# Transposing q and k on TensorE in halves of 64 columns instead of 128, in attention fused with a GEGLU block

## The chip, the cores and the metric

The kernel runs on one core of a Trainium2 chip. The metric is the device time of one launch in microseconds; the time before is the median of three runs.

## The reference

The program computes sliding-window attention with a linear distance bias (ALiBi), and then a GEGLU feed-forward block on its output. Batch 8, 8 heads, 576 positions, head size 64; 4608 tokens of width 512, hidden width 1536. All inputs and the output are float32.

```
scores = scale * q @ k.T                     # scale = 1 / sqrt(64)
mask   = (rel >= 0) & (rel < 128)            # rel = query position - key position
scores = where(mask, scores - slope[h] * |rel|, -1e9)
attn   = softmax(scores)
x      = (attn @ v), as (B*S, H*D)           # 4608 x 512
out    = (gelu(x @ w_gate) * (x @ w_val)) @ w_out
```

## The kernel before

The order of all instructions on all engines is written out by hand (a manual schedule). Everything is kept in bf16, products accumulate in float32 in PSUM, which is used as a pool of eight banks that are handed out in turn (`bank()`): a bank is free again when what reads it has finished, eight requests later.

**The feed-forward block** runs over nine groups of 512 tokens (`g`). For each group `gate_val` makes twelve hidden blocks (`f`): four matmuls with `wg` and four with `wv` (line 625, 512 moving columns each) into two banks, then ACT takes the gelu (L632) and DVE multiplies (L633). `out_part` multiplies the hidden blocks with `wo` (L662).

**Attention** for batch g+2 is set between these matmuls. POOL issues the loads of q and k (`load_qk`, L112); the sequence of a batch lies in five row blocks: four of 128 rows and one of 64 (`rows(j)`, 576 = 4 x 128 + 64), with the heads side by side, so that 128 columns are a pair of heads `c`. Scores need q and k with the head dimension on partitions. `transposes(b, c)` does this for one pair of heads: for q and for k it takes a bank, transposes the five row blocks into it (L178; the data is the weight operand and the identity moves through the array), and copies 128 x 576 elements to `qT` or `kT` (L181), q on ACT and k on DVE, but both on DVE for two pairs. One such run of five transposes is called a group here. There are 48: batches 2 to 7, four pairs, q and k.

The groups are called in blocks between other TensorE work: usually two calls, that is four groups, after a `gate_val`, with another `gate_val` behind it (f = 5 and 7 of g = 1, and f = 6 and 8 of g = 2 to 5). The first half of batch 3 follows f = 11 of g = 1, and the second half is two calls in the list of steps of g = 1 (two groups each); behind these three blocks stand scores (`score`, L209).

Batches 0 and 1 go other ways. Batch 1 is loaded in runs of rows (`RUNS`: 128 partitions with three rows each, 96 partitions with two) and is transposed by `transpose_runs` (L154), which takes 64 columns at a time and writes the two heads of a pair to rows 0 to 63 and 64 to 127 of a bank. The scores (L209, L291) and the products with the values (L494) use a quarter of the array each, 64 rows by 64 columns; the sums of L430 use 128 rows by 32 columns.

Of the kernel before, what the change touches and what calls it, by code (L numbers as in the profile page):

```python
# [32 lines left out]
def kernel(  # L33
# [10 lines left out]
    nc = tc.nc  # L44
# [23 lines left out]
    def bank():  # L68
        return psum.tile([128, 512], FP32, name="ps")
# [11 lines left out]
    ident = consts.tile([128, 128], BF16, name="ident")  # L81
# [20 lines left out]
    def rows(j):  # L102
        return 64 if j == 4 else 128
# [69 lines left out]
    def transposes(b, c, copies=None):  # L173
        for w, (src, dst, copy) in enumerate(zip((qs, ks), (qT, kT), copies or (act, dve))):
            ps = bank().bitcast(BF16)
            for j in range(5):
                n = rows(j)
                nc.tensor.transpose(  # L178
                    out=ps[:, 128 * j:128 * j + n], in_=src[b % 2][0:n, j, 128 * c:128 * c + 128],
                    identity=ident[0:n, 0:n])  # L180
            copy(out=dst[b % 2][:, c, 0:S], in_=ps[:, 0:S])  # L181


# [533 lines left out]
    for h in (0, 2, 4, 6):  # L717
        for w, src in ((0, q), (1, k)):
            (nc.scalar if w and h == 0 else nc.sync).dma_start(  # L719
                out=raw[w][h // 4].rearrange("p (h x) -> p h x", h=4)[:, h % 4:h % 4 + 2, :],  # L720
                in_=src[0][h:h + 2, 0:384, :].rearrange("h (p r) d -> p h (r d)", r=3))
# [115 lines left out]
    for do in inverse_a:  # L837
        do[1]()
    dve(out=pairs1.rearrange("p x (h d) -> p h x d", d=64),
        in_=vb[1].rearrange("p j x -> p (j x)")[:, 0:1536].rearrange(  # L840
            "p (h x d) -> p h x d", h=H, x=3))
# [46 lines left out]
    for n in range(4):  # L888
        nc.gpsimd.dma_start(
            out=wo[:, 3 * n:3 * n + 3, :],  # L890
            in_=moe_w_out[384 * n:384 * n + 384, :].rearrange("(c p) f -> p c f", p=128))
# [26 lines left out]
    def exp_table():  # L918
        nc.scalar.preload_act_table_set("natural_log_exp_and_others")

    RUN = {"s": scores, "s2": scores2, "add": add, "sum4": sums4, "gather": gather, "spread": spread_dma, "pv": values, "pv+": values_and_sums,
           "masks": flush, "table": exp_table, "transposes": transposes, "last": out_last, "scale": lambda: scales.pop()(), "o": out_half}

    for g in range(NG):
        for f in range(9 if g == 0 else 0, NF):
            gate_val(g, f)
            if g == 1 and f in (5, 7):
                transposes(2, f - 5)
                transposes(2, f - 4)
# [71 lines left out]
```

## Time and profile before

| | |
|---|---|
| median of 3 runs | 361.32 us (360.48 to 361.93) |
| the profiled execution | 361.49 us, its span 359.7 us |
| TensorE (PE) busy | 349.9 us, 97% of the span |
| its weight loads (PEld) | 184.7 us |
| DVE busy | 203.4 us |
| ACT busy | 184.4 us |
| L178: transposes of batches 2 to 7 | 240 in 13 blocks, between 68.3 and 241.4 us |
| L154: transposes of batch 1 | 80 in one block, at 36.6 us |

A row of the groups view reads: line, engine, operation, tile written <- tiles read, the part of the array (rows * columns) where it is a matmul or a weight load, the moving operand's shape, count, then busy time in us and the mean duration of one in ns, then idle time of the engine before them. A matmul's duration runs from its start to its last result, and matmuls overlap: the distance between two starts is what one costs. A piece of the chain reads: start, length, what, how many instructions.

### The profile page before, as it was taken

Reading aid. Unit: us, or ns where it says so; the run is one execution under the profiler, and the core shown is the slowest. Engines: PE = TensorE matmul, PEld = TensorE weight load, DVE = VectorE, ACT = ScalarE, POOL = GpSimd, SP = SyncE. Lnnn points to the kernel's source line nnn. Section 1 sums busy time; section 2 is a strip of 40 time slices with the busy share of each in tenths; the row PEclk is TensorE's granted clock in tenths of the full one; section 3 lists DMA queues with packets and bytes.
Section 4 is the critical chain, followed back from the end, with each engine's and each line's share of the span. In section 5 each row is a group of like instructions: output and inputs, shape, how many; then the busy total and the mean of one; then the engine's idle time right before and its main releaser. Section 6 shows DMA issues by size and latency. Waiting matters only on the chain.

```text
span 359.7 us, 8537 instructions
## 1 busy us (share of the span) xinstructions
PE 349.9 (97%) x3508; PEld 184.7 (51%) x3556; DVE 203.4 (57%) x382; ACT 184.4 (51%) x340; POOL 105.6 (29%) x139
## 2 busy tenths in 40 slices
PE   8999999999999999999999999999999999999996
PEld 6667556555654555454545554455544544444444
DVE  7887865445789546944596458844694413302420
ACT  7964786447696437544473439253753123313322
POOL 6965689406700086004900192004000000000000
PEclk9999999999999999999999999999999999999999
DMA  8999999908950099219990599049203320011002
GB/s 210 171 197 191 200 187 187 124 2 52 162 107 2 5 194 189 64 23 135 170 122 5 131 138 181 3 104 105 81 31 69 95 89 2 0 58 60 0 28 90
DMA packets 118043, 35.65 MB, mean 99 GB/s; under 512 B 101716, under 2 KB 110964, under 8 KB 118004
## 3 DMA queue, kind: packets, MB, share of 16 engines
q0 software_dynamic: 107456, 18.10, 65.2%
q1 hardware_dynamic: 7232, 10.75, 8.5%
q10 hardware_dynamic: 3316, 6.25, 7.9%
q8 instruction: 28, 0.46, 0.5%
q14 instruction: 11, 0.09, 0.1%
HBM read 43.65 MB, written 9.53 MB: 148 GB/s over the span
## 4 chain that ended last, share of the span: by engine, by line
PE 94%; DMA 1%; issue 1%; DVE 1%; ACT 1%; SPq 0%; DVEq 0%
PE ps L625 52%; PE ps L662 24%; PE ps L178 6%; PE ps L494 5%; PE ps L291 2%; PE ps L682 2%; PE ps L209 1%; DMA qs<-in_q_dram 1%; PE ps L430 1%; PE ps L698 1%; PE ps L154 1%; ACT P L222 0%; SPq L719 0%; DVE xT L530 0%; DVE qT L162 0%
## 5 line engine op out<-in xcount | busy, mean ns | idle before, releaser
L633 DVE TENSOR_TENSOR hT<-ps,gelu 128x512 bf16<-128x512 f32 (+3 forms) x117 | 73.8, 646 | 97.6 <-PE ps L625 91.3
L632 ACT ACTIVATE gelu<-ps 128x512 bf16<-128x512 f32 (+3 forms) x117 | 65.1, 564 | 98.5 <-PE ps L625 96.2
L625 PE MATMUL ps<-xT,wg 128*128 128x512 bf16 (+4 forms) x460 | 112.1, 361 | 0.8
L625 PE MATMUL ps<-xT,wv 128*128 128x512 bf16 (+4 forms) x460 | 111.2, 361 | 0.4
L662 PE MATMUL ps<-wo,hT 128*128 128x512 bf16 x374 | 87.6, 380 | 2.1 <-issue 1.4
L625 PEld LDWEIGHTS <-wv 128*128 128x128 bf16 x472 | 45.0, 98 | 48.7
L625 PEld LDWEIGHTS <-wg 128*128 128x128 bf16 x472 | 43.5, 98 | 45.8
L662 PEld LDWEIGHTS <-hT 128*128 128x128 bf16 x396 | 37.0, 98 | 43.3
L222 ACT ACTIVATE P<-ps 128x512 bf16<-128x512 f32 (+1 forms) x108 | 51.3, 583 | 3.9 <-PE ps L209 3.6
L225 DVE TENSOR_TENSOR P<-P,emask 128x768 bf16<-128x768 bf16 x60 | 31.2, 556 | 19.5 <-ACT P L222 17.7
L667 ACT COPY osb<-ps 128x512 f32<-128x512 f32 x27 | 15.9, 588 | 51.3 <-PE ps L662 51.3
L112 POOL DMA_DIRECT2D vb<-in_v_dram x40 | 34.0, 902 | 2.9 <-DMA wo<-in_moe_w_out_dram 1.0
L956 POOL COPY mark<-hT 1x2 bf16<-1x2 bf16 x4 | 0.7, 174 | 108.4 <-DVE hT L633 108.4
L112 POOL DMA_DIRECT2D qs<-in_q_dram x30 | 25.5, 870 | 4.9 <-DMA wo<-in_moe_w_out_dram 2.7
L112 POOL DMA_DIRECT2D ks<-in_k_dram x30 | 25.4, 893 | 0.3 <-PE ps L625 0.3
L181 ACT COPY qT<-ps 128x576 bf16<-128x576 bf16 x22 | 14.0, 638 | 9.8 <-PE ps L178 9.8
L494 PE MATMUL ps<-P,vb 64*64 64x192 bf16 (+2 forms) x752 | 17.7, 221 | 0.6 <-issue 0.4
L558 DVE TENSOR_TENSOR xT<-ps,rb 128x512 bf16<-128x512 f32 (+3 forms) x34 | 14.7, 502 | 4.6 <-PE ps L494 4.6
L494 PEld LDWEIGHTS <-vb 64*64 64x64 bf16 x752 | 14.7, 107 | 4.0 <-issue 3.0
L181 DVE COPY kT<-ps 128x576 bf16<-128x576 bf16 x24 | 11.0, 457 | 5.7 <-PE ps L178 5.1
L378 DVE TENSOR_TENSOR T<-P 64x1024 bf16<-64x1024 bf16 x20 | 13.7, 686 | 0.6
L178 PE MATMUL ps<-ident,ks 128*128 128x128 bf16 (+1 forms) x120 | 12.7, 218 | 0.0
(95 smaller groups left out, 238.0 us busy)
## 6 DMA issues: line engine op xcount, KB each, us to landing
out_dram<-osb SPq DMA_DIRECT2D x35, 256.0 KB, 3.1
rb<-rd ACTq DMA_DIRECT2D x10, 576.0 KB, 6.4
vb<-in_v_dram POOLq DMA_DIRECT2D x32, 128.0 KB, 6.3
qs<-in_q_dram POOLq DMA_DIRECT2D x24, 128.0 KB, 4.5
ks<-in_k_dram POOLq DMA_DIRECT2D x24, 128.0 KB, 6.1
wo<-in_moe_w_out_dram POOLq DMA_DIRECT2D x4, 384.0 KB, 12.3
wg<-in_moe_w_gate_dram POOLq DMA_DIRECT2D x5, 256.0 KB, 8.4
wv<-in_moe_w_val_dram POOLq DMA_DIRECT2D x5, 256.0 KB, 8.9
```

The lines of the kernel that those rows point to most:

```text
L112: nc.gpsimd.dma_start(out=t[at:at + n, j, :].rearrange("p (h d) -> p h d", h=H), in_=src[b][:, 128 * j:128 * j + n, :].rearrange("h p d -> ...
L178: nc.tensor.transpose(out=ps[:, 128 * j:128 * j + n], in_=src[b % 2][0:n, j, 128 * c:128 * c + 128], identity=ident[0:n, 0:n])
L181: copy(out=dst[b % 2][:, c, 0:S], in_=ps[:, 0:S])
L222: nc.scalar.activation(out=dst, in_=src, func=AF.Exp, scale=0.125)
L225: nc.vector.tensor_tensor(out=dst, in0=dst, in1=m, op=ALU.mult)
L494: mm = nc.tensor.matmul(out=out, lhsT=lhsT, rhs=prob(b)[half, c, i, col:col + q1 - q0], start=all(t[2] != u for t in todo[:n]), stop=True, ...
L558: nc.vector.tensor_tensor(out=xT[:, c, at:at + e - a], in0=src, in1=recip[b][:, c, a:e], op=ALU.mult)
L625: nc.tensor.matmul(out=ps[:, a:e], lhsT=w[:, c, 128 * f:128 * (f + 1)], rhs=xT[:, c, t0 + lo + a:t0 + lo + e], start=begins and a == 0, st ...
L632: nc.scalar.activation(out=gl[:, 0:n], in_=pg, func=AF.Gelu)
L633: nc.vector.tensor_tensor(out=hid[g][:, f, lo:hi], in0=pv, in1=gl[:, 0:n], op=ALU.mult)
L662: nc.tensor.matmul(out=acc[g], lhsT=hid[g][:, f, 128 * t:128 * (t + 1)], rhs=wo[:, f, :], start=(f == 0), stop=(f == NF - 1))
L667: (nc.vector.tensor_copy if g < B - 2 and t in by_dve.get(g, (0,)) else nc.scalar.copy)(out=osb, in_=acc[g])
```

## The change

For each row block, the one transpose of 128 columns becomes two of 64: head 2c goes to output rows 0 to 63 and head 2c+1 to rows 64 to 127. The same values land at the same places of the bank. The copies behind, the banks and the waits stay.

```diff
             ps = bank().bitcast(BF16)
             for j in range(5):
                 n = rows(j)
-                nc.tensor.transpose(
-                    out=ps[:, 128 * j:128 * j + n], in_=src[b % 2][0:n, j, 128 * c:128 * c + 128],
-                    identity=ident[0:n, 0:n])
+                for i in (0, 1):
+                    at = 128 * c + 64 * i
+                    nc.tensor.transpose(
+                        out=ps[64 * i:64 * i + 64, 128 * j:128 * j + n],
+                        in_=src[b % 2][0:n, j, at:at + 64], identity=ident[0:n, 0:n])
             copy(out=dst[b % 2][:, c, 0:S], in_=ps[:, 0:S])
```

## The prediction

> **What bounds the kernel now.** I read the page's busy shares first, then its clock row and its chain.
>
> ```profile
> PE 349.9 (97%) x3508; PEld 184.7 (51%) x3556; DVE 203.4 (57%) x382; ACT 184.4 (51%) x340; POOL 105.6 (29%) x139
> ...
> PEclk9999999999999999999999999999999999999999
> ...
> PE 94%; DMA 1%; issue 1%; DVE 1%; ACT 1%; SPq 0%; DVEq 0%
> PE ps L625 52%; PE ps L662 24%; PE ps L178 6%; PE ps L494 5%; PE ps L291 2%; PE ps L682 2%; PE ps L209 1%; DMA qs<-in_q_dram 1%; PE ps L430 1%; PE ps L698 1%; PE ps L154 1%; ACT P L222 0%; SPq L719 0%; DVE xT L530 0%; DVE qT L162 0%
> ```
>
> TensorE is busy 97% of the span at full clock and carries 94% of the chain; the two engines that empty PSUM are at 57% and 51%. The changed line, L178, is itself 6% of the chain. So what is added to or taken from TensorE in these blocks goes to the end nearly one to one. The busy column cannot say how much, since matmuls overlap: what counts is the distance from one start to the next.
>
> Next the groups by shape. L178 is the edited line; L154, batch 1's transposes, already writes 64 columns to each half of the output rows, so it is the nearest row to the new code.
>
> ```profile
> L178 PE MATMUL ps<-ident,ks 128*128 128x128 bf16 x96 | 9.5, 222 | 0.0
> L178 PE MATMUL ps<-ident,ks 64*128 64x64 bf16 x24 | 4.8, 200 | 0.0
> ...
> L154 PE MATMUL ps<-ident,qs 128*64 128x128 bf16 x24 | 1.4, 220 | 0.0
> L154 PE MATMUL ps<-ident,qs 96*64 96x96 bf16 x16 | 1.0, 205 | 0.0
> ```
>
> The first pair of numbers is the part of the array (rows * columns), the second the moving operand. A group of L178 is four transposes of shape 128*128 and one of shape 64*128 for the last 64 rows of a batch. L154 has no 64-row shape: batch 1 is loaded in runs of 128 and 96 rows.
>
> Then the chain in order of time, one block of each:
>
> ```profile
> 36.66 2.17 PE ps L154 x80
> ...
> 68.71 1.74 PE ps L178 x20
> ```
>
> L154 does eight groups (576 columns of 128 each) in 2.17 us, 0.27 us a group; L178 does four in 1.74 us, 0.43 us a group. On this view alone the edit would save 0.16 us in each of 48 groups, about 8 us. The timeline of TensorE's weight loads tells why L178 is slow:
>
> ```profile
> 68.86 0.09 PEld L178 LDWEIGHTS <-qs 64*128 64x128 bf16 x1
> 69.00 0.10 PEld L178 LDWEIGHTS <-ks 128*128 128x128 bf16 x1
> ...
> 36.59 0.11 PEld L154 LDWEIGHTS <-qs 128*64 128x64 bf16 x2 [0.42 <-issue]
> ```
>
> The fourth 128-row transpose of this group starts at 68.717. The load for the 64-row one starts 147 ns later, though loads elsewhere in the group start one step ahead; the next group's first load again waits 132 ns. The third line is the same wait where the array goes from L625's 128*128 to L154's 128*64. The starts of a group in L178 are 67, 56, 56, 151 and 132 ns apart, 462 in all, and 283 of that is going into and out of the 64-row shape. The 128-row transposes come every 56 ns; L154's pairs also come every 55 to 56 ns, the second of a pair 2 to 5 ns after the first. A pair does the work of one old transpose, so **for 128-row blocks the edit gains nothing**.
>
> **The change part by part.** *The shape switch.* I went through every place in the trace where the shape of the array changes between two matmuls, and took the distance between their starts:
> - 128*128 to 64*128 (rows only) after 128 moving columns: 150 to 151 ns, 48 times
> - 64*128 to 128*128 after 64 columns: 129 to 133
> - 64*128 to 64*64 (columns only) after 64 columns: 129 to 130 (L178 to L209), 121 (L790 to L494)
> - 64*64 to 128*128: 121 to 123 after 64 columns where nothing else is waited for, 149 after 128
> - 128*128 to 64*64, 128*32 or 128*64 after 512 columns: 308 to 310, against 216 without a change
> - 96*64 to 128*128 after 96 columns: 137.
>
> Subtract the streaming time (216 ns for 512 columns, so 27 for 64 and 54 for 128), and each is 93 to 106 ns: the array empties whenever rows or columns of the shape change. From 128*64 to 96*64 nothing is paid (51 to 53 ns). The new code goes from 128*64 to 64*64 for the last 64 rows of each group and back. That pair is not in the trace. From below its cost is that of 128*64 to 96*64, nothing; from above 151 in and 131 out. I take 151 in and 122 out (the row of 64*64), because a change of rows alone pays at 128 columns in each of the 48 groups.
>
> The Trainium skill speaks against the edit here: "TensorEngine Tiling (Array Packing)", Key Properties, says that changing the mode, not only the tile, drains TensorE, and its list has 128x64 and 64x64 as different modes. By that rule the sum is the one made here; without it, the faster rival's below. No run before shows that pair.
>
> *One new group.* First pair at 0. The second pair comes 79 ns later, as in L154 after its switch (36.590 to 36.669); L178 has 67 there. Then 56 and 56: fourth pair at 191, its second half at 194. Switch of 151: the 64-row pair at 345 and 348. Switch out of 122: next group at **470 ns against 462**, 8 more.
>
> *Entering a block.* Before, L625 or L662 goes into L178 at the normal 216, with no change of shape. Now it goes to 128*64: 309, the L154 row. That is 93 more for each block.
>
> *Blocks.* There are 13: eleven of four groups, two of two. Ten return to L625: before 216 + 1704 + 132 = 2052 ns from the last matmul ahead to the first behind; new 309 + 4 x 470 = 2189; 137 more, **1.37 us** for ten. One of four groups goes on to the scores of L209, whose shape is 64*64: before 2051, new 309 + 1880 less the last switch (122 becomes 27) = 2094, 43 more. The two of two groups, also to L209: 1126 before, 309 + 940 - 95 = 1154 new, 28 more each. **Sum 1.37 + 0.04 + 0.06 = 1.47 us.**
>
> *Doubled instructions.* 240 more loads and 240 more matmuls. L154 issues 160 of both in 2.03 us, 12.7 ns each, so their number does not bind. A load of 64 columns takes 106 to 113 ns in L154, against 91 to 100 in L178; both are already inside the distances used. The skill's "TensorE: Matmul & The Clock Gate", section LDWEIGHTS, has load time fall with columns (64 would take half of 128); the rows disagree. By it the 79 could fall to 56, and the sum to 0.4 us.
>
> *Copies and banks.* The copies at L181 (ACT 638 ns, DVE 457 ns) read the same 576 columns and number the same. Each waits for the last transpose of its group, a few ns to 0.2 us later than now; ACT now sits idle 0.3 to 0.6 us before each for that reason. Their four banks are taken again by the third gate_val after the block, two gate_vals of 1.7 us later, which hides the delay; without that cover a copy's 0.64 us would fall on TensorE. No DMA, and no instruction on ACT, DVE, POOL or SP, is added or moved. Loads and stores start from the same instructions, slightly later.
>
> The profiled execution took 361.49 us (span 359.7), 0.17 above the median of 361.32. 361.49 + 1.47 = **363.0 us**.
>
> **Rivals.** *Faster: the column-halved shapes do not drain among themselves.* For it: 128*64 to 96*64 costs nothing. Against it: rows-only and columns-only changes both pay everywhere else, and 96 rows may simply count as the full height. Then a group is L154's 256 ns. Ten blocks: 309 + 4 x 256 + 94 (switch out for the usual last step) = 1427, 625 less each, 6.25 us; the block to L209 0.72 less; the two short ones 0.31 each. Together 7.6 us less: 353.9. It decides if the 64*64 load starts while the fourth pair still streams.
>
> *Slower by more: the 64-row pair does not overlap.* Both halves read rows 0 to 63. If the second follows only after the first has streamed, 27 ns more in 48 groups make 1.3 us; with a switch out of 131 instead of 122, another 0.43. Sum up to 3.2 us: 364.7. Against it: L154's pairs also share their rows and overlap.
>
> *No effect.* Later TensorE work falls into some wait. The chain has 1% of DMA, nearly all of it one load at 2 to 7 us, and L178 has no idle time before it: 361.5.
>
> **How the numbers follow.** The drain with overlapping pairs gets 0.64, the dearer drain 0.20, no drain 0.10, no effect 0.06. The likeliest lies between 0.9 us (67 instead of 79 in each group: 0.6 less) and 1.9 us (10 ns more a group: 0.5 more). The bound of 0.5%, 1.8 us, is about what a measurement of this kernel can tell from no change; runs before spread over 360.48 to 361.93, so about 0.26 of the 0.64 falls above it. Slower: 0.26 + 0.20 = 0.46. Same: 0.38 + 0.06 = 0.44. Faster: 0.10. The range runs from 361.6 (1.47 less the spread and the cheaper step) to 364.9 (the dear drain), and leaves out the fast case.
>
> **What would show it.** Right: in the profile after, the 64-row transposes have shape 64*64, their first load starts about 147 ns after the fourth pair, groups are 470 ns apart, and each block is entered at 309 ns. L178's share of the chain grows slightly. Wrong: 64*64 loads right behind the fourth pair and groups of about 256 ns (faster), halves of the 64-row pair 27 ns or more apart (slower by more), or TensorE waiting for a bank after the block.

## The result and the profile after

The changed kernel takes **363.65 us** (median of 4 runs, 363.36 to 364.31) against 361.28 before (4 runs, 360.48 to 361.93). The ratio is 1.0076 with a 95% interval of 1.0053 to 1.0098: slower by 2.37 us by the medians, 1.9 to 3.5 us by the interval, in the forecast direction, 0.65 us above the forecast of 363.0 and inside the range. The profiled execution took 363.36 us, span 361.6. The edit moved L178 to L180 and all later lines by two.

The page after: busy shares, clock and chain.

```profile
PE 355.3 (98%) x3796; PEld 185.3 (51%) x3796; DVE 204.2 (56%) x382; ACT 184.3 (51%) x340; POOL 105.6 (29%) x139
...
PEclk9999999999999999999999999999999999999999
...
PE 96%; DMA 1%; DVE 1%; ACT 1%; issue 1%; SPq 0%; DVEq 0%
PE ps L627 52%; PE ps L664 24%; PE ps L180 7%; PE ps L496 5%; PE ps L293 2%; PE ps L684 2%; PE ps L211 1%; DMA qs<-in_q_dram 1%; PE ps L432 1%; PE ps L700 1%; PE ps L154 1%; ACT P L224 0%; SPq L721 0%; DVE qT L162 0%; ACT rb L578 0%
```

TensorE still carries the chain at full clock; the edited line grew from 6% to 7% of it. DVE and ACT do the same number of instructions as before in the same busy time to within 0.8 us, POOL in the same time.

The groups by shape:

```profile
L180 PE MATMUL ps<-ident,ks 128*64 128x128 bf16 x192 | 9.9, 225 | 0.0
L180 PE MATMUL ps<-ident,ks 64*64 64x64 bf16 x48 | 5.2, 213 | 0.0
...
L180 PEld LDWEIGHTS <-qs 128*64 128x64 bf16 x192 | 6.1, 109 | 6.0 <-issue 5.5
L180 PEld LDWEIGHTS <-qs 64*64 64x64 bf16 x48 | 2.6, 103 | 2.2
```

The shapes are the ones forecast. Two things are new: the 5.5 us in which the weight loads stood idle at the entry of the 13 blocks, and a 64*64 matmul of 213 ns. It lasts longer than the 64*128 one that it replaces (200).

The timeline of the weight loads at the first block:

```profile
68.12 0.11 PEld L180 LDWEIGHTS <-qs 128*64 128x64 bf16 x1 [0.42 <-issue]
...
68.46 0.11 PEld L180 LDWEIGHTS <-qs 64*64 64x64 bf16 x2
68.61 0.14 PEld L180 LDWEIGHTS <-ks 128*64 128x64 bf16 x4
```

The block is entered with the idle 0.42 us that L154 had. The 64-row loads start at 68.461, 148 ns behind the fourth pair's second half (68.313): the price of a change of shape is paid between 128*64 and 64*64 too. The next group's load starts 141 ns behind the second 64-row transpose (68.466).

Start to start, against the forecast (a pair is the two halves of one row block), the same in all 48 groups and 13 blocks to within 2 ns:

| step | forecast, ns | measured, ns |
|---|---|---|
| last matmul to the first pair (block entry) | 309 | 309 |
| first pair to the second | 79 | 80 |
| second to third, third to fourth | 56 | 56 |
| second half of a pair behind the first | 3 | 3 to 4 |
| fourth pair into the 64-row pair | 151 | 149 |
| 64-row pair to the next group | 122 | **143** |
| 64-row pair to the feed-forward work | 122 | **146** |
| a group | 470 | **491** |

A block of four groups that returns to the feed-forward work: 309 + 1820 + 146 = 2275 ns (2052 before, 2189 forecast). Ten of them make 2.23 us; the four-group block that goes to the scores 309 + 1821 + 6 = 2136 against 2051, 0.09; the two short ones 309 + 838 + 7 = 1154 against 1126, 0.06 together. **The sum is 2.37 us, and the medians differ by 2.37.** That the two agree to the last digit is chance, since the interval of the measured difference is 1.6 us wide. The two profiled executions differ by 1.87 only, since in the one after, the first block starts 0.52 us earlier relative to before (68.118 against 68.549, with 0.09 of entry added): the work ahead of the edited code differs by that much between these two executions.

### The profile page after: what moved, and what is told of

Same layout as the page of the kernel before. It is cut to its first block, busy times and chain, and to the rows that moved or that the text cites. A ratio compares the mean times of both kernels' runs of the same rounds, so it can differ in the third digit from the quotient of the medians.

```text
span 361.6 us, 9065 instructions
## 1 busy us (share of the span) xinstructions
PE 355.3 (98%) x3796; PEld 185.3 (51%) x3796; DVE 204.2 (56%) x382; ACT 184.3 (51%) x340; POOL 105.6 (29%) x139
## 4 chain that ended last, share of the span: by engine, by line
PE 96%; DMA 1%; DVE 1%; ACT 1%; issue 1%; SPq 0%; DVEq 0%
PE ps L627 52%; PE ps L664 24%; PE ps L180 7%; PE ps L496 5%; PE ps L293 2%; PE ps L684 2%; PE ps L211 1%; DMA qs<-in_q_dram 1%; PE ps L432 1%; PE ps L700 1%; PE ps L154 1%; ACT P L224 0%; SPq L721 0%; DVE qT L162 0%; ACT rb L578 0%
## 5 line engine op out<-in xcount | busy, mean ns | idle before, releaser
L627 PE MATMUL ps<-xT,wv 128*128 128x512 bf16 (+4 forms) x472 | 112.7, 361 | 0.0
L664 PE MATMUL ps<-wo,hT 128*128 128x512 bf16 x396 | 90.4, 380 | 0.4 <-issue 0.4
L183 ACT COPY qT<-ps 128x576 bf16<-128x576 bf16 x22 | 14.1, 639 | 12.0 <-PE ps L180 12.0
L183 DVE COPY kT<-ps 128x576 bf16<-128x576 bf16 x24 | 11.0, 457 | 8.2 <-PE ps L180 8.2
L180 PE MATMUL ps<-ident,qs 128*64 128x128 bf16 (+1 forms) x240 | 13.5, 223 | 0.0
```

What stands on the lines that cost most here:

```text
L180: nc.tensor.transpose(out=ps[64 * i:64 * i + 64, 128 * j:128 * j + n], in_=src[b % 2][0:n, j, at:at + 64], identity=ident[0:n, 0:n])
L627: nc.tensor.matmul(out=ps[:, a:e], lhsT=w[:, c, 128 * f:128 * (f + 1)], rhs=xT[:, c, t0 + lo + a:t0 + lo + e], start=begins and a == 0, st ...
L664: nc.tensor.matmul(out=acc[g], lhsT=hid[g][:, f, 128 * t:128 * (t + 1)], rhs=wo[:, f, :], start=(f == 0), stop=(f == NF - 1))
```

## The experiments

**One half of the change and the other.** The theory: each change of the array's shape empties TensorE, and the blocks' time is streaming plus such changes. The rivals: halving costs something for every transpose; twice the instructions cost time as such.

Row blocks of 128 rows in halves, the 64-row block whole (the edit is shown against the changed kernel, the time is compared with the kernel before):

```diff
-                for i in (0, 1):
-                    at = 128 * c + 64 * i
+                for at, w in (((0, 64), (64, 64)) if j < 4 else ((0, 128),)):
                     nc.tensor.transpose(
-                        out=ps[64 * i:64 * i + 64, 128 * j:128 * j + n],
-                        in_=src[b % 2][0:n, j, at:at + 64], identity=ident[0:n, 0:n])
+                        out=ps[at:at + w, 128 * j:128 * j + n],
+                        in_=src[b % 2][0:n, j, 128 * c + at:128 * c + at + w], identity=ident[0:n, 0:n])
```

> Half of the change: the four row blocks of 128 rows in halves of 64 columns, the 64-row block whole as before (64*128). Theory: 309 ns into each of 13 blocks, a group of 476 ns (0, 79, 135, 191, pair 194, then 151 into the 64-row shape and 131 out of it); the exits to the scores still change the shape. Sum 2.0 us more than before, near 363.3 us. Rival (what is new in cost is the pair in the 64*64 shape): about 1.2 us more, from the entries alone.

Measured: 362.92 us against 361.09, ratio 1.0051 (1.0030 to 1.0072). Entry 309 ns, 80 to the second pair, 152 into the 64-row shape and 129 to 130 out: blocks of 2217 ns, by the sum of the starts 2.1 us. The other half has `j == 4` in place of `j < 4`:

> The other half: the four row blocks of 128 rows whole as before, the 64-row block as two halves (64*64). Theory: blocks are entered at 216 ns as before; groups of 477 ns against 462 (144 instead of 131 out of the 64-row shape, 3 for the second half); three exits to the scores no longer change the shape and give back about 0.13 us each. Sum 0.3 us more than before, near 361.6 us. With the other half this makes the measured change, 2.4 us. Rival (halving as such is what costs, wherever): a fifth of the change, 0.5 us more, and as much for each of the five row blocks.

Measured: 361.72 us, ratio 1.0018 (1.0004 to 1.0031), so 0.65 us with an interval of 0.14 to 1.1. Entry 216 ns, 149 into 64*64, 145 to 146 out: blocks of 2112 ns; the three exits to the scores come 6 to 7 ns behind the last transpose, where 129 to 130 stood before. By the sum of the starts this is 0.30 us. The medians lie 1.83 and 0.63 above the kernel before, together 2.46 where the whole change measures 2.37.

The times alone do not decide: the 1.2 us of the first rival and the 0.5 us of the second lie within the intervals. The starts do. Pairs of 128 rows in halves come every 56 ns, as whole transposes do, so halving as such costs nothing there; what is added stands at the entry, at the first pair behind it and at the changes of shape. The 0.3 us by which the second time exceeds its sum lies within its noise. Its profiled execution also holds a wait of 0.86 us among the scores (L292, at 100.7 us) that the one before does not have; its cause is not shown.

**No 64-row shape at all.** The last row block is taken as 96 rows, 32 of which are padding that is never read behind the transpose:

```diff
-                n = rows(j)
+                n = 96 if j == 4 else 128
...
     load_qk(2)
+    for t in (qs[0], ks[0]):
+        nc.gpsimd.memset(t[64:96, 4, :], 0.0)
```

In the kernel before:

> Whole transposes of 128 columns as before, but the last row block of a batch is taken as 96 rows instead of 64 (32 rows of padding, whose transposed columns nobody reads), so that its shape is 96*128. Theory (each change of the array's shape empties TensorE, and the blocks' time is streaming plus such changes): no change of shape inside a block, a group of 4 x 56 + 42 = 266 ns instead of 462; a block of four groups that returns to the feed-forward work costs 216 + 1064 = 1280 ns instead of 2052. Sum about 9.0 us less than before, near 352.3 us. Rival (transposes with the identity as moving operand are slow in themselves, or the copies out of PSUM set the pace): less than 2 us gained.

Measured: **352.6 us, ratio 0.9762 (0.9742 to 0.9781)**. Its groups and its weight loads in the same block:

```profile
L178 PE MATMUL ps<-ident,qs 128*128 128x128 bf16 x96 | 9.3, 219 | 0.0
L178 PE MATMUL ps<-ident,qs 96*128 96x96 bf16 x24 | 5.0, 208 | 0.0
```

```profile
68.79 0.31 PEld L178 LDWEIGHTS <-ks 128*128 128x128 bf16 x5
69.06 0.31 PEld L178 LDWEIGHTS <-qs 128*128 128x128 bf16 x5
69.33 0.31 PEld L178 LDWEIGHTS <-ks 128*128 128x128 bf16 x5
69.60 0.14 PEld L625 LDWEIGHTS <-wg 128*128 128x128 bf16 x2
```

The loads of successive groups start 0.27 us apart, where they stood 0.46 apart before. Larger transposes were faster: a block is 216 + 1034 + 47 = 1297 ns instead of 2052, and TensorE has no wait that it did not have before. By the starts the saving is 8.8 us, by the medians 8.5.

In the changed kernel, with `n` the same:

> The changed kernel (halves of 64 columns), with the last row block taken as 96 rows, so that no 64*64 shape is left. Theory of the shape changes: 309 ns into a block, pairs every 56 ns with 79 once after the entry, 137 out; a block of four groups 1491 ns against 2052 before: about 6.5 us less than before, near 354.8 us; pairs inside a block 56 ns apart. Rival (twice the instructions cost time by themselves, 2.4 us for 240 pairs, 10 ns for each added load and matmul): pairs some 66 ns apart, and little better than before the padding than by what the rest says, near 357 us.

Measured: 355.09 us, ratio 0.983 (0.981 to 0.985). Behind the step of 80 ns at the entry, pairs come 54 ns apart on average (about 47 behind a 96-row pair, 55 to 59 elsewhere), and whole transposes with the same padding come as far apart: 20 loads and 20 matmuls more per block cost nothing between its ends. What the halves cost over the whole transposes is the way in (309 against 216), the first pair (80 against 56) and the way out (140 against 47), 210 ns a block and 2.5 us in the medians. The rival of the doubled instructions falls.

**Fewer changes of shape, same shapes.** All 128-row transposes of a block first, then the 64-row ones, then the copies; a call now takes all groups of a block and its banks at the start:

```diff
+        for js in (range(4), (4,)):
+            for c, src, dst, copy, ps in todo:
+                for j in js:
...
+        for c, src, dst, copy, ps in todo:
+            copy(out=dst[b % 2][:, c, 0:S], in_=ps[:, 0:S])
```

> Whole transposes of 128 columns, as before, in another order: of all groups of a block first the 128-row transposes, then the 64-row ones, then the copies. The shape changes once in and once out of the 64-row shape for each block instead of once for each group. Theory: 216 + 15 x 56 + 151 + about 137 for the four 64-row ones + 131 = 1475 ns for a block of four groups instead of 2052 (up to 1660 if their loads do not run ahead); about 6.5 us less than before, near 354.6 us, at most 356.5. Rival (the 64-row transposes are slow in themselves, not the change to them): no gain, and four distances of 130 to 150 ns between them.

Measured: 354.7 us, ratio 0.9815 (0.9791 to 0.9839). The four 64-row transposes of the first block:

```profile
69.31 0.20 PE L183 MATMUL ps<-ident,qs 64*128 64x64 bf16 x1
69.35 0.19 PE L183 MATMUL ps<-ident,ks 64*128 64x64 bf16 x1
69.38 0.19 PE L183 MATMUL ps<-ident,qs 64*128 64x64 bf16 x1
69.41 0.19 PE L183 MATMUL ps<-ident,ks 64*128 64x64 bf16 x1
```

They follow each other after 39, 29 and 29 ns: they are not slow in themselves. One way in (152) and one out (122 to 123) are left of four each in a block. The same order with the halves:

> The changed kernel's halves in the same order: all 128-row pairs of a block, then all 64-row pairs. Theory: 309 + 867 + 149 + about 136 for four pairs + 122 out = 1583 ns for a block instead of 2275 in the changed kernel; near 355.6 us, 8 us under the changed kernel. The way out is 122 ns, not 146, since the last of four pairs has its weights loaded ahead. Rival (leaving 64*64 after 64 columns costs 146 whatever stands before): 146 ns.

Measured: 356.23 us, ratio 0.9853 (0.9830 to 0.9877). The way out to the feed-forward work is 125 ns, where a single pair has 146. The pairs of 64 rows follow each other after 53, 32 and 31 ns.

**The mis-sized step.** In the changed kernel the 64-row pair is issued twice, into the same place:

```diff
-            for j in range(5):
+            for j in (0, 1, 2, 3, 4, 4):
```

> The changed kernel with the 64-row pair of each group issued twice, into the same place. Theory (a matmul right behind a change of shape takes some 23 ns longer since its weights are not loaded ahead, and with a single pair this is paid on the way out): the second pair comes about 79 ns behind the first, lasts 190 ns instead of 213, and the way out behind it is 122 ns instead of 143; a group 550 ns instead of 491, 2.8 us more in all than the changed kernel, near 366.5 us. Rival (the way out of 64*64 to 128*64 costs 143 whatever stands before it): 143 again, 3.8 us more, near 367.5 us.

Measured: 365.27 us, ratio 1.0104 (1.0076 to 1.0133), 1.6 us above the changed kernel (1.5 by the starts). The way out is 122 to 124 ns to the next group in all 35 places, and 125 to the feed-forward work. The second pair follows 53 ns behind the first, not 79, so a group is 522 ns and the sum smaller than expected. Its loads start 26 ns ahead of it (its matmuls at 69.068), while those of the next group again start with their matmuls:

```profile
69.04 0.11 PEld L180 LDWEIGHTS <-qs 64*64 64x64 bf16 x2
69.19 0.11 PEld L180 LDWEIGHTS <-ks 128*64 128x64 bf16 x2
```

The groups by shape, for this kernel and for the one with all 64-row pairs in a row:

```profile
L180 PE MATMUL ps<-ident,qs 64*64 64x64 bf16 x96 | 6.0, 203 | 0.0
```

```profile
L183 PE MATMUL ps<-ident,qs 64*64 64x64 bf16 x48 | 3.5, 204 | 0.0
L183 PE MATMUL ps<-ident,ks 64*64 64x64 bf16 x48 | 3.2, 193 | 0.0
```

Issued twice, the mean of 203 is one pair of 213 and one of 193. In the other kernel only q has the pair that stands first behind the change of shape; the k pairs behind it last 193. The first matmul after a change is the long one, and with a single pair it is also the last. The 20 ns are not saved by a second pair: they leave the way out and turn up in the step from the first pair to the second, 53 ns where later pairs in a row take 31 or 32.

## Why the prediction was right, and the step that was off

- **TensorE bounds the kernel, and the blocks go to the end one to one.** Right: the starts sum to 2.37 us and the medians differ by 2.37 (1.9 to 3.5). In three faster kernels (both padded ones and the whole transposes in the new order) the starts give 8.8, 6.3 and 7.3 us less than before, the medians 8.5, 6.0 and 6.9.
- **Nothing to gain in the 128-row blocks.** Right: a pair and a whole transpose both take 56 ns. The reading of the chain that would have given 8 us (0.27 us a group in L154, 0.43 in L178) compared a block without the 64-row shape with one that has it.
- **128*64 to 64*64 drains.** Right: 149 ns in all 48 places. The choice rested on a row of L178, where a change of rows alone pays, and it came out. (That row read 150 to 151 ns; in the trace it is 150 to 153.) The trace agrees with the Trainium skill's "TensorEngine Tiling (Array Packing)", Key Properties, by which a change of tiling mode drains TensorE. The faster rival falls: its condition, a 64*64 load while the fourth pair streams, never occurs.
- **The load rule of the Trainium skill's "TensorE: Matmul & The Clock Gate", section LDWEIGHTS.** By this rule a load of 64 columns takes half as long as one of 128. Here the two took 109 ns (128*64) and 97 ns (128*128, before). The step behind the entry stayed at 80, and the sum of 0.4 us that the rule gave is not borne out.
- **The pair overlaps.** Right, 3 to 4 ns apart, so the mechanism of the slower rival did not occur. Its other term, a dearer way out, did.
- **The way out of the 64-row shape was the term that was mis-sized**: 122 forecast, 143 and 146 measured. I took the 122 from stays of many matmuls in 64*64, whose last one had its weights loaded ahead. Here the stay is a single pair, whose matmuls start within 2 ns of their own loads and last 213 ns instead of 193. 21 ns in 35 places between groups and 24 in ten exits are 0.98 us; three exits to the scores come 6 ns behind instead of 27, 0.06 back; the step of 80 and the way in (149, not 151) about cancel. That is 0.9 us, and 1.47 + 0.9 = 2.37. The upper bound had held 131 for this step, so it was too low too. The prediction's own list had the sign of it: the same change from 64*128 to 64*64 cost 129 to 130 ns behind the single transposes of L178 (200 ns each), and 121 behind L790, which has 24 in a row (191). And its step of 79 instead of 56 behind the entry is the same extra for the 128*64 pair (243 ns against 219); for the 64-row pair it was put at nothing. That the late load makes the first matmul longer is not shown apart from the change of shape: in these traces the two come together.
- **The copies and banks hide.** Right as far as the trace shows: TensorE's matmuls have no idle time before L180 (0.0 in the groups), and the copies at L183 are not among the chain's lines. In the nine places where a block that returns to the feed-forward work is followed by another, the starts of the two lie 213 to 226 ns further apart than before, near the 223 that the block itself takes more: nothing is added behind it.
- **How near it was.** Partly luck. The forecast of 363.0 adds its 1.47 us to the profiled execution (361.49), which lay 0.21 above the median before; so the miss is 0.65 us in the time and 0.90 in the rise. The rise of 2.37 lies above the 0.9 to 1.9 us that the prediction held likeliest, and the time is inside the range because the range reaches to the dear drain, whose main term (pairs that do not overlap) did not occur.

The fastest of the versions is the kernel before with the last row block padded to 96 rows: 352.6 us, 2.4% less than before.

## What to carry to other kernels

Where TensorE sets the end, list its matmuls with the shape of the array (rows * columns) and count how often the shape changes: here each change cost 93 to 119 ns beyond the streaming of the last matmul, more than the 27 or 54 ns for which a transpose of 64 or 128 rows streams. Keep a shape for long, by padding a short block to the height of its neighbours or by putting all short blocks together, before making pieces smaller: halving a transpose gained nothing here, since a pair takes as long as the one transpose that it replaces. When a price is taken from a row, check that the matmul ahead of it stood in the same place: first behind a change of shape, or in a stream.

## What the runs showed of the hardware

- 96 rows count as the full height: 128*128 to 96*128 costs 56 ns and back 47, 128*64 to 96*64 about 55 and back 46 to 47; from 96*64 to 128*128 it is 140 and from 96*128 to 64*64 137.
- Within these runs the distance over a change of shape is the last matmul's duration less some 70 ns: 219 gives 149, 200 gives 130, 213 gives 143, 193 gives 122, 380 gives 309. In a stream of one shape it is the duration less some 160: 219 gives 56, 243 gives 80, 193 gives 32, 213 gives 53. So the longer first matmul behind a change is paid on whichever step follows it. The profile models the ends of matmuls, so the starts are the firmer numbers.
- Twice as many loads and matmuls in the same time: pairs in 128*64 kept the 56 ns of one whole transpose with 20 instructions of each kind more in a block.
